# Attention feeding a mixture of experts on one core: batch loads over iterations, slot sums and lead products in another order, a separate home for late rows, two gathers sooner

## The chip, the core and the metric

The kernel runs on one core of a Trainium2 chip. The metric is the device time of one execution in microseconds. The engines named below are TensorE (PE; its weight loads are shown as PEld), VectorE (DVE), ScalarE (ACT), GpSimd (Pool) and SyncE (SP), which here only issues DMAs.

## What is computed

A chunked linear attention with decay, over 4 batches, 8 heads, 768 positions, whose output goes, row by row, to one of 8 experts. Cut to what matters:

```python
# attention, per batch and head, chunk by chunk
cum = cumsum(log(a))
y = (C @ B.T * exp(cum_i - cum_j) * causal) @ x + (C @ state) * exp(cum)
state = exp(sum(log a)) * state + sum_j(B_j x_j * exp(cum_last - cum_j))
# mixture of experts over the 3072 rows of 256 of y
logits = y @ w_gate                  # 256 x 8
e = argmax(logits); gate = softmax(logits)[e]
slot = rows so far that chose e      # kept if below the capacity of 768
out[row] = gate * (relu(y[row] @ w1[e]) @ w2[e])   # 256 -> 1024 -> 256
```

## The kernel before

The order of the instructions of every engine is written out by hand; engines wait for each other by semaphores that the framework sets from the tiles that they read and write. A tile pool gives a buffer again when its last readers are done, and memory of a pool that is closed goes to pools opened later, whose tiles then wait for the old ones' readers.

**Attention** (up to L874) works on 24 tiles of 128 positions, six per batch, in the loop over `k`. Iteration `k` makes the score products of tile `k` (`scores`, L441, from `b_n` and `cbd`, a block form of `c_n`) and masks them, turns the finished rows of tile `k - 2` (`rows_of`, `stage_c`: transposes L480, logits L484, copies to `rt` L498 and of the logits L485), multiplies tile `k - 1` (`intra` L462, `inter` L473) and carries the state (`carry` L401). The loads of batch `b + 1` are spread over the six iterations of batch `b` by `load_part(b + 1, t)` (L341), all on SP's queue: at `t = 0` `bt` and `cn`, at `t = 1` `bn` and the first part of `x`, at `t = 2` six loads of decay rows (L220) and four of blocks of `cn` into `cbd` (L353), at `t = 3` the second part of `x`. `paced` (L337) makes a load wait for the decay product of the next tile. `make_bp(k + 2)` reads `b_s`, `make_ct(k + 2)` reads `c_n`. From iteration 10 on SP also loads the raw weights of experts 0 and 1.

**Routing** is done for groups of tiles (4, 4, 4, 4, 4, 3, 1): `route_1` on DVE finds the best expert, `route_2` counts on TensorE, `route_3` makes slot numbers and one-hot matrices (`hot_a`, `hot_e`, `hot_b`), and `listed` or `list_` (L832) sums row numbers into the table of slots. `who` (L851) is the finished table. `rt` rows with the gate behind them go to DRAM, `rows_d` (L577).

**The lead** is a block of 128 rows of expert 0, known after the first 12 tiles and gathered during attention. At attention's end it is turned (`lead_turn`, L621: two transposes L156, each followed by a copy L625) and multiplied by expert 0's `w1` in four products of 8 matmuls (`lead_gemm`, L630, matmuls L636, Relu L637): one before the last groups' counts, one behind the first `list_`, two before the last `list_`. Its second product is L1100, and eight matmuls of no use (L1105) fill the time behind it.

**Experts** (`experts`, L883) run in eight units; unit 0 is the rest of expert 0 (296 rows), the others have 424. Rows are fetched by indirect DMAs on Pool in blocks of 128 (`gather`, L893, `fetch`, L169) into buffers `g`, three of them in the pool `gp`, which is opened when attention's pools are closed. Unit 0's three blocks are fetched at once; unit 1's four one by one, the block `f` after the matmuls of column block `f` of unit 0's first product (`gemm1`, L983, L990). Then `turned` transposes the rows of the next unit on TensorE (units 0 and 1) or on DVE (the others), between the two products of the unit before (`gemm2`, L1007). `hp` holds `hh` and `hl`, the two halves of the intermediate; `hl`'s buffer holds `x` of batches 0 and 2 during attention. The gate of a row is read in `put` (L1040) from column 256 of `g`. Weights of the expert after next are loaded behind matmuls of `gemm1`.

## Time and profile before

| what | us |
|---|---|
| median of 3 runs | 272.77 |
| lowest, highest | 272.13, 274.0 |
| the profiled execution | 274.5 |
| its span, first to last instruction | 272.6 |
| TensorE busy | 250.5 (92%) |
| DVE, Pool, ACT busy | 177.0, 130.4, 128.1 |

The profile is of one execution. Its rows name an engine, a line of the kernel and what an instruction writes and reads, as `ps<-xh,wh`. "Idle before" is time in which the engine did nothing ahead of an instruction, with what released it. "issue" marks time in which the engine waited for nothing that the profile shows. [...] Busy time of TensorE is modelled and holds pipelined matmuls.

### The profile page before, as it was taken

Reading aid. Unit: us, or ns where it says so; the run is one execution under the profiler, and the core shown is the slowest. Engines: PE = TensorE matmul, PEld = TensorE weight load, DVE = VectorE, ACT = ScalarE, POOL = GpSimd, SP = SyncE. Lnnn points to the kernel's source line nnn. Section 1 sums busy time; section 2 is a strip of 40 time slices with the busy share of each in tenths; the row PEclk is TensorE's granted clock in tenths of the full one; section 3 lists DMA queues with packets and bytes.
Section 4 is the critical chain, followed back from the end, with each engine's and each line's share of the span. In section 5 each row is a group of like instructions: output and inputs, shape, how many; then the busy total and the mean of one; then the engine's idle time right before and its main releaser. Section 6 shows DMA issues by size and latency. Waiting matters only on the chain.

```text
span 272.6 us, 7096 instructions
## 1 busy us (share of the span) xinstructions
PE 250.5 (92%) x2747; PEld 208.3 (76%) x2747; DVE 177.0 (65%) x437; ACT 128.1 (47%) x289; POOL 130.4 (48%) x165
## 2 busy tenths in 40 slices
PE   7799999969999996979999999999999999999960
PEld 3246556635557884979999999999999999999960
DVE  6699597846896852565686587478488676766210
ACT  2377457547755251455373373274284554643000
POOL 6975234324691232634466567467444475015230
PEclk9999999986999598999999999999999999999996
DMA  6583536935746401494762773773865815101010
GB/s 190 163 248 91 149 113 196 308 84 126 195 148 189 155 10 38 150 363 160 205 256 86 181 297 101 192 302 112 243 242 147 356 41 166 36 2 62 20 43 5
DMA packets 30101, 42.06 MB, mean 154 GB/s; under 512 B 16089, under 2 KB 22075, under 8 KB 28528
## 3 DMA queue, kind: packets, MB, share of 16 engines
q1 hardware_dynamic: 26656, 33.69, 39.5%
q0 software_dynamic: 3280, 7.86, 9.2%
q8 instruction: 23, 0.38, 0.6%
q14 instruction: 14, 0.11, 0.2%
q10 hardware_dynamic: 128, 0.01, 0.0%
HBM read 32.19 MB, written 9.39 MB: 153 GB/s over the span
## 4 chain that ended last, share of the span: by engine, by line
PE 80%; DMA 6%; DVE 5%; issue 3%; ACT 1%; POOL 1%; POOLq 0%; SPq 0%; DVEq 0%
PE ps L983 26%; PE ps L1007 20%; PE sp L441 5%; PE yp L462 4%; PE ps2f L1065 4%; PE yp L473 3%; PE pj L480 3%; DMA r<-w 3%; DMA g<-rows_d,who 3%; PE dsp L401 3%; PE lead_p L636 2%; PE psy L1053 2%; PE ldp L391 2%; PE yp L411 1%; PE warm L304 1%
## 5 line engine op out<-in xcount | busy, mean ns | idle before, releaser
L169 POOL DMA_INDIRECT g<-rows_d,who x31 | 49.9, 1610 | 44.4 <-PE ps L1007 31.7
L986 DVE SCALAR_TENSOR_TENSOR hl<-ps,hh 128x424 fp32r<-128x424 f32 (+1 forms) x64 | 37.1, 582 | 32.3 <-ACT hh L985 32.3
L985 ACT ACTIVATE hh<-ps 128x424 fp32r<-128x424 f32 (+1 forms) x64 | 32.7, 512 | 46.4 <-PE ps L983 46.4
L1041 POOL DMA_INDIRECT out<-yo,oi x31 | 30.6, 987 | 33.1 <-DVE yo L1040 33.1
L1007 PE MATMUL ps<-hh,wh 128*128 128x424 f32 (+1 forms) x112 | 39.0, 348 | 0.0
L1007 PE MATMUL ps<-hh,wl 128*128 128x424 f32 (+1 forms) x112 | 38.8, 347 | 0.0
L1007 PE MATMUL ps<-hl,wh 128*128 128x424 f32 (+1 forms) x112 | 38.8, 347 | 0.0
L983 PE MATMUL ps<-xh,wh 128*128 128x424 f32 (+1 forms) x128 | 37.6, 375 | 0.2 <-ACT xh L945 0.2
L128 DVE TENSOR_TENSOR wl<-r,wh 128x1024 fp32r<-128x1024 f32 (+1 forms) x32 | 34.9, 1146 | 0.8 <-ACT wh L127 0.8
L983 PE MATMUL ps<-xh,wl 128*128 128x424 f32 (+1 forms) x128 | 35.3, 355 | 0.1
L983 PE MATMUL ps<-xl,wh 128*128 128x424 f32 (+1 forms) x128 | 34.7, 352 | 0.0
L127 ACT ACTIVATE wh<-r 128x1024 fp32r<-128x1024 f32 (+2 forms) x48 | 34.2, 765 | 0.1
L983 PEld LDWEIGHTS ps<-xh,wl 128*128 128x128 f32 x128 | 24.3, 194 | 1.3 <-DVE wl L128 0.7
L983 PEld LDWEIGHTS ps<-xl,wh 128*128 128x128 f32 x128 | 24.2, 192 | 0.6
L983 PEld LDWEIGHTS ps<-xh,wh 128*128 128x128 f32 x128 | 22.2, 194 | 0.8 <-ACT xh L945 0.4
L1007 PEld LDWEIGHTS ps<-hl,wh 128*128 128x128 f32 x112 | 21.1, 188 | 0.6
L1007 PEld LDWEIGHTS ps<-hh,wh 128*128 128x128 f32 x112 | 21.1, 188 | 0.4
L1007 PEld LDWEIGHTS ps<-hh,wl 128*128 128x128 f32 x112 | 21.0, 188 | 0.4
L475 ACT ACTIVATE ys<-yp 128x128 f32<-128x128 f32 x48 | 10.7, 275 | 20.7 <-PE yp L473 20.7
L447 DVE TENSOR_TENSOR mz<-sp,lx 128x512 f32<-128x512 f32 x24 | 16.5, 687 | 4.5 <-PE sp L441 4.0
L366 POOL TENSOR_TENSOR bpt<-b_s,wt 128x128 f32<-128x128 f32 x22 | 10.0, 456 | 17.5 <-PE dsp L401 17.4
L462 PEld LDWEIGHTS yp<-mz,xz 128*32 128x32 f32 x768 | 12.6, 112 | 5.4 <-issue 2.9
(185 smaller groups left out, 438.0 us busy)
## 6 DMA issues: line engine op xcount, KB each, us to landing
r<-w SPq DMA_DIRECT2D x12, 1024.0 KB, 6.1
r<-w SPq DMA_DIRECT2D x16, 256.0 KB, 4.0
g<-xr_d SPq DMA_DIRECT2D x24, 112.0 KB
rows_d<-rt SPq DMA_DIRECT2D x5, 514.0 KB
xr_d<-g SPq DMA_DIRECT2D x6, 385.5 KB
xz<-x SPq DMA_DIRECT2D x6, 256.0 KB, 4.2
b_s<-bt SPq DMA_DIRECT2D x3, 384.0 KB, 3.1
c_n<-cn SPq DMA_DIRECT2D x3, 384.0 KB, 3.8
```

The source lines that it names most:

```text
L127: act.activation(hi[:, sl], r[:, sl], AF.Copy)
L128: engine.tensor_tensor(out=lo[:, sl], in0=r[:, sl], in1=hi[:, sl].bitcast(F32), op=ALU.subtract)
L169: got = pool.indirect_dma_start(out=g[0:r, s], out_offset=None, in_=rows_d[0:known, :], in_offset=bass.IndirectOffsetOnAxis(ap=index[0:r, ...
L441: pe.matmul(sp[64 * c:64 * c + 64, g, 0:4 * CH], nat(b, "bn", ts.start, ts.stop)[gp], cbd[b % 2][gp, :, ts], start=True, stop=True)
L447: dve.tensor_tensor(out=m.rearrange("p (g h) i -> p g h i", g=2), in0=sp[:, :, 0:4 * CH].rearrange("p g (h i) -> p g h i", h=4), in1=lx.re ...
L462: step[0] = pe.matmul(yps[g][32 * hh:32 * hh + 32, c * CH:(c + 1) * CH], x_z[:, c, h * D:(h + 1) * D], m[:, h], start=c == 0, stop=False, ...
L983: mm = pe.matmul(ps, wv[:, k, fs], xv[:, k], start=i == 0, stop=i == 5)
L985: act.activation(hh[:, f, 0:w], ps, AF.Relu)
L986: dve.scalar_tensor_tensor(out=hl[:, f, 0:w], in0=ps, scalar=0.0, in1=hh[:, f, 0:w].bitcast(F32), op0=ALU.max, op1=ALU.subtract)
L1007: mm = pe.matmul(ps, wv[:, f, ds], hv[:, f, 0:w], start=f == 0 and j == 0, stop=f == NF - 1 and j == 2)
L1041: sc = pool.indirect_dma_start(out=out, out_offset=bass.IndirectOffsetOnAxis(ap=oi[0:r, s:s + 1], axis=0), in_=yo[0:r], in_offset=None, bo ...
L1065: pe.matmul(ps, hv[:, f, sl], wv[:, f, :], start=f == 0 and j == 0, stop=f == NF - 1 and j == 2)
```

## The change

In `load_part`, `cn` stays at `t = 0`, `bt` goes to `t = 1` and `bn` to the end of `t = 2`. In `stage_c`, for the tiles of the last two groups, the copies of the logits go ahead of the copy of the rows. `lead_turn` is called before the rows of tile 21 are turned, and its two copies are run after tile 23's `inter`; of the four lead products one stands ahead of the rows of tile 22, one ahead of the turn of the last tile, one where it stood behind the first `list_`, and one behind the counts (`cnt`). Unit 0's gathered rows get a tile in `hp` with the tag `hl`. The gate is copied to a small tile of its own in `turned`. Two of unit 1's four gathers are issued behind unit 0's, the other two behind column blocks 0 and 1.

```diff
--- before.py
+++ after.py
@@ -339,7 +339,7 @@
             follow(dma.ins, beat[0], "not all loads at once")
 
         def load_part(b, t):
-            for nm in ((("bt", "cn"), ("bn",)) + ((),) * 4)[t]:
+            for nm in ((("cn",), ("bt",)) + ((),) * 4)[t]:
                 paced(out=loads[b][nm], in_=src_of[nm][:, b])
             if t in (1, 3):
                 load_xz(b, t // 2, pace=True)
@@ -351,6 +351,7 @@
                     for g in range(2):
                         r = slice(64 * g + N * i, 64 * g + N * (i + 1))
                         sp_.dma_start(out=cbd[b % 2][r, i], in_=cn[r, b])
+                paced(out=loads[b]["bn"], in_=bn[:, b])
             if t in (3, 4):
                 expand(b, t - 3, 0, S, act)
 
@@ -495,8 +496,8 @@
                 r = lgs.shape[0]
                 pe.transpose(out=pj[:, 384:384 + r], in_=lgs, identity=ident[0:r, 0:r])
                 after.append(lambda: act.activation(Ls, pj[:, 384:384 + r].rearrange("p (j e) -> p j e", e=32)[:, :, 0:E], AF.Copy))
-            act.activation(rt[:, i, 0:DM], pj[:, 0:DM], AF.Copy)
-            for f in after:
+            late = [lambda: act.activation(rt[:, i, 0:DM], pj[:, 0:DM], AF.Copy)]
+            for f in after + late if direct else late + after:
                 f()
 
         def stage_c_last(ys, rt):
@@ -618,11 +619,11 @@
             numbers(lead_t["slot"], slice(0, 1))
             fetch(lead_t["g"], lead_t["slot"], lead, LEAD * P)
 
-        def lead_turn():
+        def lead_turn(stored):
             both = p1.tile([P, 2, 512], F32, name="lead_ps", tag="sp", bufs=2)
             banks = [both[:, k] for k in range(2)]
             turn(lead_t["g"], lead, lambda w: banks.pop(0)[:, 0:w],
-                 lambda k, ps: act.activation(lead_t["x"][:, k], ps, AF.Copy))
+                 lambda k, ps: stored.append(lambda: act.activation(lead_t["x"][:, k], ps, AF.Copy)))
             pool.tensor_copy(lead_t["gate"], lead_t["g"][:, 0, GATE:GATE + 1])
 
         lead_f = list(range(0, NF if lead else 0, 2))
@@ -788,19 +789,22 @@
         sb[k - 1] = inter(yps, cts.pop(k - 1), sa.pop(k - 1))
         for f in lots:
             f()
-        early = take()
+        early, stored = take(), []
+        if lead:
+            lead_turn(stored)
         rows_of(k - 2, k)
         early += take()
         yps, lots = intra(x_of(k), ms.pop(k), sa[k], None, hots)
         sb[k] = inter(yps, cts.pop(k), sa.pop(k))
         for f in lots:
             f()
+        for f in stored:
+            f()
         side.extend(early)
         settle_due(k + 1)
         early = take()
         assert not due and not hots
-        if lead:
-            lead_turn()
+        lead_gemm()
         rows_of(k - 1, k)
         mid = take()
         rt = sm.tile([P, 1, ROW], F32, name="rt_last", bufs=1)
@@ -809,6 +813,7 @@
             pe.matmul(lg, sb[k][:, g], wg[:, g, 0:E], start=g == 0, stop=g == 1, skip_group_check=True)
         last = route_last(k, rt, lg)
         late = take()
+        lead_gemm()
         pj = p1.tile([P, 512], F32, name="pj_last", tag="y")
         turn_rows(pj, sb.pop(k))
         act.activation(rt[:, 0, 0:DM], pj[:, 0:DM], AF.Copy)
@@ -819,7 +824,6 @@
         settled = sm.tile([P, E * ks], F32, name="settled")
         numbers(settled, slice(0, E * ks))
         weave(mid, [lambda: None, lambda: None] + late)
-        lead_gemm()
         mid = route_2(*due.pop()[1], at_of(1, 4 * E)[:, 0:3 * E].rearrange("p (t e) -> p t e", e=E))
         route_3(*mid)
         mid = take()
@@ -844,8 +848,6 @@
         hots.append(hot(*known[0], pool))
         hots.append(hot(*known[1], dve))
         known.clear()
-        while lead_f:
-            lead_gemm()
         while hots:
             list_(*hots.pop(0))
         dve.tensor_tensor(out=who, in0=settled, in1=spots, op=ALU.add)
@@ -853,6 +855,8 @@
         got = sm.tile([P, 2 * E], F32, name="got")
         for i, r in enumerate((runs[0], lead_run)):
             pe.matmul(cnt[:, i * E:(i + 1) * E], ones, r, start=True, stop=True)
+        while lead_f:
+            lead_gemm()
         act.activation(got, cnt, AF.Copy)
         most = sm.tile([P, 1], F32, name="most")
         late = sm.tile([P, 1], F32, name="late")
@@ -890,9 +894,9 @@
             ph = mt.enter_context(tc.tile_pool(name="ph", bufs=3, space=PSUM))
             py = mt.enter_context(tc.tile_pool(name="py", bufs=2, space=PSUM))
 
-            def gather(e, w0, w, most):
+            def gather(e, w0, w, most, home=None):
                 blocks = -(-w // P)
-                g = gp.tile([P, blocks, ROW], F32, name="g", bufs=3)
+                g = home.tile([P, blocks, ROW], F32, name="g_first", tag="hl") if home else gp.tile([P, blocks, ROW], F32, name="g", bufs=3)
 
                 def block(s, *pace):
                     fetch(g, who[:, e * ks + w0 // P:(e + 1) * ks], most, only=(s,), pace=pace)
@@ -958,7 +962,11 @@
                     act.activation(xh, xt[:, :, 0:w], AF.Copy)
                     dve.tensor_tensor(out=xl, in0=xt[:, :, 0:w], in1=xh.bitcast(F32), op=ALU.subtract)
                 if not rare:
-                    gate = g[:, :, GATE]
+                    gate = gp.tile([P, -(-w // P)], F32, name="gate")
+                    full = w // P
+                    for s0, n, r in ((0, full, P), (full, 1, w % P)):
+                        if n and r:
+                            dve.tensor_copy(gate[0:r, s0:s0 + n], g[0:r, s0:s0 + n, GATE])
                 gone = dead[:, e]
                 if rare:
                     gone = gp.tile([P, -(-w // P)], I32, name="gone")
@@ -1084,13 +1092,16 @@
             size = lambda u: units[u][2] if u < 2 else -(-units[u][2] // Q) * Q
             g, g_n, now = None, None, []
             if not rare:
-                g, now = gather(*first, size(0))
+                g, now = gather(*first, size(0), hp)
             for job in now:
                 job()
             ahead_g, four = {}, {}
             if len(units) > 1:
                 ahead_g[1], more = gather(*units[1], size(1))
                 rows_.extend(more)
+            if not rare:
+                for _ in range(2):
+                    rows_.pop(0)()
             after = []
             if ahead:
                 yt = gp.tile([P, 2, lead], F32, name="yt", bufs=1)
```

## Rows read from the trace of the kernel before

**Rows 1.** The page, part 4: the chain that ended last, by engine.

```profile
PE 80%; DMA 6%; DVE 5%; issue 3%; ACT 1%; POOL 1%; POOLq 0%; SPq 0%; DVEq 0%
```

**Rows 2.** The chain in order of time, attention; columns: start us, us, what.

```profile
34.80 0.59 PE sp L441 x8
...
54.64 0.59 PE sp L441 x8
...
56.66 2.52 issue
...
68.48 0.59 PE sp L441 x8
```

**Rows 3.** Stretches: length; busy PE, PEld, DVE, ACT, POOL; clock; DMA share, GB/s.

```profile
47.00:56.00 9.00, 9.00 (x224) 5.44 (x226) 7.32 (x25) 5.36 (x19) 3.16 (x8) 1.00 0.94 282
...
57.00:58.00 1.00, 0.00 (x0) 0.00 (x0) 0.21 (x2) 0.00 (x0) 0.16 (x1) 1.00 0.05 7
58.00:59.00 1.00, 0.00 (x0) 0.00 (x0) 0.00 (x0) 0.00 (x0) 0.00 (x0) 1.00 0.08 12
...
59.20:66.00 6.80, 6.80 (x104) 3.63 (x104) 3.06 (x12) 3.98 (x13) 1.67 (x4) 0.50 0.53 133
...
90.00:96.70 6.70, 6.24 (x40) 5.85 (x40) 4.59 (x32) 1.36 (x5) 1.03 (x3) 0.50 0.29 98
103.00:106.30 3.30, 1.38 (x6) 0.75 (x6) 0.00 (x0) 0.42 (x1) 0.94 (x1) 1.00 0.18 52
107.00:110.00 3.00, 3.00 (x13) 3.00 (x14) 1.27 (x6) 0.46 (x2) 1.03 (x1) 0.50 0.01 3
...
117.00:118.00 1.00, 0.48 (x4) 0.44 (x4) 0.00 (x0) 0.20 (x1) 0.00 (x0) 1.00 1.21 361
```

**Rows 4.** The page, part 3: the queue that brings instructions.

```profile
q8 instruction: 23, 0.38, 0.6%
```

**Rows 5.** Timeline of DVE: start us, us, line, op; what ended its idle time.

```profile
94.55 0.33 DVE L596 TENSOR_TENSOR hot_b<-hot_e,cb_s 128x48 bf16<-128x48 bf16 x2
97.37 0.20 DVE L851 TENSOR_TENSOR who<-settled,spots 128x48 int32<-128x48 f32 x1 [2.50 <-PE cnt L855]
...
98.73 0.15 DVE L869 TENSOR_TENSOR load<-late,most 128x1 int32<-128x1 f32 x1
```

**Rows 6.** Timeline of TensorE, attention's end and expert 0.

```profile
46.26 0.74 PE L441 MATMUL sp<-cbd,b_n 64*64 64x256 f32 x8
...
91.94 5.17 PE L636 MATMUL lead_p<-lead_h,r 128*128 128x128 f32 x24
...
97.68 3.83 PE L1100 MATMUL ps<-lead_h,r 128*128 128x128 f32 x32 [0.33 <-ACT got L856]
101.34 1.62 PE L1105 MATMUL warm<-cb_s 128*128 128x432 bf16 x8
...
106.86 0.60 PE L983 MATMUL ps<-xh,wh 128*128 128x296 f32 x1 [0.15 <-ACT xh L945]
...
115.16 0.81 PE L156 MATMUL ps<-hd_s,g 128*128 128x128 f32 x3
117.52 0.92 PE L156 MATMUL ps<-hd_s,g 40*128 40x40 f32 x5 [1.55 <-DMA g<-rows_d,who]
```

**Rows 7.** Timeline of Pool: first gather of expert 0, last of expert 1.

```profile
99.74 1.60 POOL L169 DMA_INDIRECT g<-rows_d,who  x1 [5.29 <-ACT wh L127]
...
112.80 0.99 POOL L169 DMA_INDIRECT g<-rows_d,who  x1 [0.30 <-PE ps L983]
```

**Rows 8.** Timeline of SP's DMA queue in attention.

```profile
40.03 2.01 SPq L353 DMA_DIRECT2D cbd<-cn  x4
...
50.84 0.46 SPq L338 DMA_DIRECT2D b_n<-bn  x1
```

**Rows 9.** The DMA issues by line: count, KB each, median us to landing.

```profile
c_n<-cn SPq DMA_DIRECT2D x3, 384.0 KB, 3.8
...
xz<-x SPq DMA_DIRECT2D x6, 128.0 KB, 6.8
```

## The prediction

> **What bounds the kernel now.** I read the page first: the chain of work that ended last is TensorE for 80% of the span [rows 1], so a change pays only where TensorE stands still or runs at the lower of its two clock levels. Then I looked for such places, in the chain in order of time, in the table of stretches, and in the timelines of the engines around each. There are three.
>
> The first is in attention. Score products start on average every 2.83 us: from 34.80 to 54.64, seven iterations, 19.84 us. The next three take from 54.64 to 68.48, 13.84 us, where 3 x 2.83 = 8.49 were due: 5.35 us are lost [rows 2]. Of these, 2.52 us are a standstill marked "issue", in which TensorE waits for no semaphore. In the nine microseconds before it the DMA engines are 94% busy; in it they do almost nothing (7 and 12 GB/s) [rows 3]. 7 plus 12 KB is about one packet of the "instruction" queue: 0.38 MB in 23 packets is 16.5 KB each [rows 4]. I read this as code that TensorE is short of, whose transfer had stood behind the data until they were through. After it the clock is 0.50 (1.2 GHz) from 59.2 to 66 us [rows 3]; the other 5.35 - 2.52 = 2.83 us (by chance the same figure) are put down to that.
>
> The second place is the end of attention. DVE has the last one-hot product ready at 94.88 (94.55 + 0.33), but `who`, the table of which row sits in which expert's slot, is added only at 97.37 [rows 5], because 24 matmuls of the lead block stand before the last slot sums in TensorE's order, from 91.94 [rows 6]. The gather of expert 0's rows begins later still, at 99.74 [rows 7]. Its target lies in memory that attention's pools have to give back, and the last instruction that reads one of those small tiles is `load<-late,most`, which ends at 98.88 [rows 5], 0.86 us before. TensorE runs out of work, is busy for 1.38 of 3.30 us, and falls to 0.50 for the first matmuls of expert 0 [rows 3].
>
> The third is between the two products of expert 0: the turn of expert 1's rows starts at 115.16, and its last block, whose gather began at 112.80, is there at 117.52, after 1.55 us of waiting [rows 6, 7]. From 118.4 on TensorE is full, one expert after the other; what is won before stays won unless weights or rows are late.
>
> **The change, part by part.** The profiled execution took 274.5 us (span 272.6); the median of the runs is 272.77, 1.7 less. The terms are differences, taken from the profiled execution and subtracted from the median.
>
> *Loads spread.* At the batch's first iteration `cn` is loaded alone, `bt` moves to the second, where `bn` was, and `bn` to the third, behind six row loads and four block loads on SP. Nothing is added or removed: three loads of 384 KB per batch. What changes is the heap that the code packet stands behind. Before, `bt` and `cn` were issued together and `bn` behind them at 50.84 [rows 8]; afterwards `bt` goes there, and one load of 384 KB fewer is ahead. At the 282 GB/s of that stretch [rows 3] this is 1.36 us; I take 1.2, since part of the time was less than full. The standstill falls from 2.52 to about 1.3 us. An idle of 1.55 us before 117.52 left the clock at 1.00 [rows 3, 6], so at 1.3 us I take it as kept, and the 2.83 us come back too: 4.0 us. The ends are 0 (the heap does not matter) and 5.35 (no standstill).
>
> [...] The row says that the packet came only when the data were through [rows 3]. [...]
>
> What this costs: `bn` is late by design. In batch 1 the block loads end at 42.04 [rows 8]; `bn` goes next, and the like-sized `cn` lands 3.8 us after issue [rows 9], thus at 45.9; the first product that reads it starts at 46.26 [rows 6]. That is no slack to speak of. By the 6.8 us of the slowest kind of load [rows 9] it would be at 48.9 and TensorE would stand 2.6 us. I take the near row and charge 0.3 us for all three batches (ends 0 and 2.6 for each of two). Stores of rows, `x` and weights queued behind it on SP start 0.4 us later and have more slack than that.
>
> *Slot sums ahead of lead products.* The four lead products (8 matmuls each) are spread: one before the rows of tile 22 are turned, one before the last tile's, one where it was, one after the counts. At the higher clock 32 such matmuls take 3.83 us [rows 6], so a product is 0.96; at the lower, 24 in 5.17, so 1.72. The routing chain on DVE has one product ahead of it that was not there, and two small copies on ACT; the copy of the logits now goes ahead of the copy of the rows, which gives a part back. I charge the chain 1.0 us (ends 0 and 1.9): the last one-hot at 95.9 instead of 94.88, `who` complete at 96.45 instead of 97.57. The slot sums no longer queue.
>
> *A home of their own.* Expert 0's gathers go into the `hl` buffer, free since batch 2's `x` was used, and so wait for `who` and the stored rows only. With Pool's 0.86 us from release to start, the first begins at 97.3 instead of 99.74: 2.4 us earlier, and the last block is there at 105.55 - 2.4 = 103.1. TensorE's own work: counts at 96.2, a lead product 0.96, 0.33 of waiting for ACT, then 3.83 and the filler 1.62 [rows 6], thus 102.9. Both sides meet, so I take 2.4 (ends: 0 with TensorE late, 3.0).
>
> With no gap there is no fall of the clock. From 106.86 to 115.16 stand 48 matmuls and two small ones, 8.30 us [rows 6]; of this 3.0 us at least run at 0.50 [rows 3]. Work at half the clock takes twice its time, so half of the 3.0 would come back, 1.5; I take 1.3, as a short gap may be left (ends 0 and 1.7).
>
> *Expert 1's gathers forward.* Two of four follow expert 0's three directly, the others after the first and second column block of its first product instead of the third and fourth. Pool does the same gathers in the same order. The last leaves some 2.5 us earlier in relation to the product, before expert 1's weights are asked for. The 1.55 us of waiting go; it can't give more (lower end 0). The later blocks then queue behind nothing on Pool.
>
> *Gate copies.* Two small DVE copies per unit, some 0.15 us each like those of [rows 5], lie beside matmuls; DVE is busy for 177.0 of 272.6 us: 0. Without that cover they would cost 8 x 0.3 = 2.4 us. They set the gathered rows free one unit earlier.
>
> Sum: -4.0 + 0.3 - 2.4 - 1.3 - 1.55 = -8.95 us; 272.8 - 8.95 = 263.8 us.
>
> **The rivals.**
>
> *The heap does not matter.* The code packet is late for another reason, or is served in turn with the data and simply asked for late, and the 5.35 us stay. For it: a standstill named "issue" has no releaser in the profile. Against: it lies right behind the fullest nine microseconds of attention [rows 3]. The time is 263.8 + 4.0 = 267.8. [...]
>
> *Lead products run at the lower clock.* Before, the clock was 0.50 from 90 to 96.7 us [rows 3]. If it falls likewise, one product costs the chain 0.76 us more, the one after the counts 0.76 more, and the 32 matmuls up to 3.1 more: TensorE is ready at 107.5 instead of 102.9, 2.0 us behind where the last rows came before. Then 2.4 are not won but 2.0 lost: 268.2. Against it: two of the four now stand before 90 us, where it fell, and make TensorE's work there denser.
>
> *`bn` late* (the other side). If its transfer lands after 6.8 us instead of 3.8, batches 1 and 2 both begin with about 2.6 us of standstill, and each pulls the clock down as at 59 us, another 2.83: 2 x 5.4 = 10.9 us against 9.25 won, thus 272.8 - 9.25 + 10.9 = 274.4. It turns the sign from a landing of 6.0 us on; from 7.4 us on, 0.6 more in each of the two batches, the time is over 275.5. For it: its place on SP; against it: `cn` of the same size lands in 3.8 us [rows 9].
>
> *Given back.* Experts 2 to 7 have to wait for weights by what was won: 272.8. Against it: those loads are issued after matmuls, and so move with them.
>
> **How the numbers follow.** Forecast 0.52; heap 0.20 (the cause is read from two rows, not from a releaser); lower clock 0.12; given back 0.07; `bn` late 0.09, two thirds of it with the longer landing, as standstills add up. The number is that of the forecast. Its own range is 261.5 to 266: the low end is no standstill at all (1.35 more) and 3.0 for the home (0.6 more), 261.9 and a little; the high end is half of one of the large terms gone. The first two rivals, at 267.8 and 268.2, are taken in, with one microsecond on top: 261.5 to 269.5 leaves the last two out, and some of the others' tails. About 1% is what a measurement can tell from no change: faster than 270.0 are the first three, 0.84; within 1% "given back" and a third of `bn` late, 0.10; slower the rest of that, 0.06.
>
> **What would show it.** Right: a chain with no or a shorter "issue" piece near 56 us and a clock of 1.00 there; `bn` loads landed before scores of tiles 6, 12 and 18; `who` near 96.5 and the first gather within 1 us of it, both moved by what attention gains; no lower clock in expert 0's first product; no wait for DMA at expert 1's turn. Wrong: a standstill as long as before; a gather that still starts behind `load<-late,most`; lead products at 1.7 us each; a new wait for `b_n`; a wait for weights behind expert 1.

## The result: 1.1% faster, a third of what was forecast

The changed kernel takes 269.52 us (median of 20 runs, 268.27 to 274.97), the kernel before in the same runs 273.07. The ratio of the times is 0.9887, 95% interval 0.9855 to 0.9919, so 3.1 us where 8.95 were forecast; 269.52 lies just above the range. In two later jobs the ratio was 0.9878 and 0.989. All ratios are to the kernel before in the same job. (Of most kernels here some executions show a lower mean clock and are longer, of the changed one four of 20 with 0.947 to 0.959 and 273.33 to 274.97 us; ratios, and averages over "undisturbed" profiles, leave them out, medians do not.)

The profiled execution took 269.67 us, span 267.9. Its chain by engine, to be held against [rows 1]:

```profile
PE 80%; DVE 7%; DMA 3%; issue 3%; ACT 2%; POOL 1%; SPq 0%; POOLq 0%; ACTq 0%; DVEq 0%
```

The chain in order of time, attention (start us, us, what), against [rows 2]:

```profile
24.55 4.12 DMA b_n<-bn
28.80 0.78 PE sp L442 x8
...
46.30 1.15 issue
...
52.76 1.36 issue
...
69.93 0.45 issue
...
85.75 0.48 issue
```

The standstill at 56.66 is gone, but four shorter ones stand elsewhere, and `bn` is on the chain, which it was not. They add up to 3.4 us against 2.52 before (a piece of 0.75 to 0.87 near 75, which both have, left out).

The one at 46.30 ends with the first score product of tile 12, which reads the `bn` loaded for its batch:

```profile
42.53 1.04 SPq L338 DMA_DIRECT2D b_n<-bn  x1
...
47.42 0.36 PEld L442 LDWEIGHTS sp<-cbd,b_n 64*64 64x64 f32 x8 [1.21 <-issue]
```

No view names its releaser, but the trace's semaphore records do: the semaphore of this load makes its last step at 47.36, 0.06 us before the weight load. So 1.15 of the 3.4 us are a wait for `bn`, and the other three pieces, 2.3 us, stand against the 2.52 of before.

TensorE at the end of attention and in expert 0, against [rows 6]:

```profile
95.52 2.05 PE L637 MATMUL lead_p<-lead_h,r 128*128 128x128 f32 x8
98.12 5.23 PE L1111 MATMUL ps<-lead_h,r 128*128 128x128 f32 x32 [0.55 <-ACT got L860]
103.19 1.62 PE L1116 MATMUL warm<-cb_s 128*128 128x432 bf16 x8
104.65 1.12 PE L156 MATMUL ps<-hd_s,g_first 128*128 128x128 f32 x6
105.72 0.95 PE L991 MATMUL ps<-xh,wh 128*128 128x296 f32 x2
...
113.04 1.33 PE L156 MATMUL ps<-hd_s,g 128*128 128x128 f32 x8
114.30 0.41 PE L1015 MATMUL ps<-hh,wh 128*128 128x296 f32 x1
```

DVE, against [rows 5]:

```profile
95.05 0.33 DVE L597 TENSOR_TENSOR hot_b<-hot_e,cb_s 128x48 bf16<-128x48 bf16 x2
95.67 0.20 DVE L853 TENSOR_TENSOR who<-settled,spots 128x48 int32<-128x48 f32 x1 [0.29 <-PE cnt L857]
99.19 0.15 DVE L873 TENSOR_TENSOR load<-late,most 128x1 int32<-128x1 f32 x1
```

Pool's gathers, against [rows 7]:

```profile
97.27 1.07 POOL L169 DMA_INDIRECT g_first<-rows_d,who  x1 [2.32 <-issue]
...
99.95 1.15 POOL L169 DMA_INDIRECT g_first<-rows_d,who  x1 [0.30 <-DVE lead_oi L876]
...
108.80 0.99 POOL L169 DMA_INDIRECT g<-rows_d,who  x1 [0.30 <-issue]
```

Stretches (length; busy PE, PEld, DVE, ACT, POOL; clock; DMA share, GB/s), against [rows 3]:

```profile
88.00:94.20 6.20, 4.79 (x50) 4.38 (x49) 5.91 (x42) 2.08 (x8) 1.07 (x3) 1.00 0.35 117
94.20:101.10 6.90, 5.74 (x32) 5.29 (x32) 4.17 (x19) 2.53 (x6) 3.97 (x5) 0.51 0.28 88
...
105.00:113.00 8.00, 7.85 (x55) 7.35 (x55) 4.90 (x16) 3.75 (x9) 2.85 (x3) 1.00 0.36 103
```

The gathers begin at the time that was forecast (97.3), no longer behind `load<-late,most`, and neither expert's turn waits for a row. That it is just this time is luck: it was to move with attention, which gained 0.65 us, and from the end of `who` (95.87) to the first gather it is 1.40 us where 0.86 were taken. And TensorE is late: the clock is 0.50 from 94.2 to 101.1 (a share of the full clock; no trace here shows it in GHz), two lead products pay for it, and expert 0's rows are turned only at 104.65.

Cut at four points, the two profiled executions differ as follows; the rows below the first are distances between neighbouring points. The last tile's score product and expert 0's first product, before:

```profile
82.98 0.66 PE L441 MATMUL sp<-cbd,b_n 64*64 64x256 f32 x8
...
106.31 0.40 PE L983 MATMUL ps<-xh,wh 128*128 128x296 f32 x1
```

and the last tile's score product after:

```profile
82.33 0.66 PE L442 MATMUL sp<-cbd,b_n 64*64 64x256 f32 x8
```

```
stretch                                          before   after   differs  forecast
start to the last tile's score product            82.98   82.33    -0.65     -3.7
  to expert 0's first product                     23.33   23.39    +0.06     -2.4
  to the turn of expert 1's rows                   8.85    7.32    -1.53     -1.3
  to expert 0's second product                     3.20    1.26    -1.94     -1.55
  to the end of the time                         156.14  155.37    -0.77      0
```

Nearly all that is missing in these two executions lies in the first two lines, 3.05 and 2.46 us. The experiments ask why.

### The profile page after: what moved, and what is told of

Its sections match the earlier page's. It is cut to its first block, busy times and chain, and to the rows that moved or that the text cites. A ratio compares the mean times of both kernels' runs of the same rounds, so it can differ in the third digit from the quotient of the medians.

```text
span 267.9 us, 7098 instructions
## 1 busy us (share of the span) xinstructions
PE 246.7 (92%) x2746; PEld 206.3 (77%) x2747; DVE 178.6 (67%) x453; ACT 127.6 (48%) x289; POOL 126.5 (47%) x165
## 4 chain that ended last, share of the span: by engine, by line
PE 80%; DVE 7%; DMA 3%; issue 3%; ACT 2%; POOL 1%; SPq 0%; POOLq 0%; ACTq 0%; DVEq 0%
PE ps L991 27%; PE ps L1015 23%; PE sp L442 4%; PE ps2f L1073 4%; PE yp L463 4%; PE yp L474 3%; PE pj L481 2%; PE psy L1061 2%; PE dsp L402 2%; PE ps L1111 2%; DMA b_n<-bn 2%; PE ldp L392 1%; DMA c_n<-cn 1%; DVE mz L448 1%; PE yp L412 1%
## 5 line engine op out<-in xcount | busy, mean ns | idle before, releaser
L169 POOL DMA_INDIRECT g<-rows_d,who x28 | 42.7, 1527 | 37.3 <-PE ps L1015 32.6
L991 PE MATMUL ps<-xh,wh 128*128 128x424 f32 (+1 forms) x128 | 36.9, 368 | 0.1
L991 PE MATMUL ps<-xh,wl 128*128 128x424 f32 (+1 forms) x128 | 34.2, 348 | 0.0
L991 PE MATMUL ps<-xl,wh 128*128 128x424 f32 (+1 forms) x128 | 34.1, 348 | 0.0
L991 PEld LDWEIGHTS ps<-xl,wh 128*128 128x128 f32 x128 | 23.6, 188 | 0.7
L991 PEld LDWEIGHTS ps<-xh,wl 128*128 128x128 f32 x128 | 23.6, 188 | 0.6
L991 PEld LDWEIGHTS ps<-xh,wh 128*128 128x128 f32 x128 | 21.6, 189 | 0.8 <-ACT xh L949 0.4
L448 DVE TENSOR_TENSOR mz<-sp,lx 128x512 f32<-128x512 f32 x24 | 16.5, 686 | 5.3 <-PE sp L442 3.7
L442 PE MATMUL sp<-cbd,b_n 64*64 64x256 f32 x176 | 15.5, 401 | 2.0 <-issue 1.6
```

The source lines that it names most:

```text
L169: got = pool.indirect_dma_start(out=g[0:r, s], out_offset=None, in_=rows_d[0:known, :], in_offset=bass.IndirectOffsetOnAxis(ap=index[0:r, ...
L442: pe.matmul(sp[64 * c:64 * c + 64, g, 0:4 * CH], nat(b, "bn", ts.start, ts.stop)[gp], cbd[b % 2][gp, :, ts], start=True, stop=True)
L448: dve.tensor_tensor(out=m.rearrange("p (g h) i -> p g h i", g=2), in0=sp[:, :, 0:4 * CH].rearrange("p g (h i) -> p g h i", h=4), in1=lx.re ...
L991: mm = pe.matmul(ps, wv[:, k, fs], xv[:, k], start=i == 0, stop=i == 5)
```

## Experiments on the loads

**The kernel before once more, and each half alone.** No edit in the first. In the second, the kernel before with only the loads spread:

```diff
-            for nm in ((("bt", "cn"), ("bn",)) + ((),) * 4)[t]:
+            for nm in ((("cn",), ("bt",)) + ((),) * 4)[t]:
...
                         sp_.dma_start(out=cbd[b % 2][r, i], in_=cn[r, b])
+                paced(out=loads[b]["bn"], in_=bn[:, b])
```

In the third, the changed kernel with the reverse edit.

> The kernel before, unchanged, for a second profiled execution. Theory: the 2.52 us standstill at 56.66 and the lower clock behind it were one draw of when a packet of TensorE's code got through the full DMA queue, not a fixed cost of the bunched loads. Then this execution shows a standstill of another size or at another place, and the score product of the last tile (82.98 in the first profile) starts 1 to 3 us away from that. Rival (the bunched loads cost this each time): again a standstill of over 2 us between 54 and 59, TensorE at the lower clock behind it, the last tile's score product within 0.7 us of 82.98. Either way expert 0's second product starts 35 to 39 us behind that score product, and the total is 271 to 277 us.

> The kernel before with only the loads spread (cn, then bt, then bn behind the ten row and block loads). Theory: the spread trades one wait for others; the late bn holds the first score product of tile 12 for about 1.2 us and that of tile 6 for 0.5, and what stands behind it on SP makes a later code packet late; score products of the last tile start within 1 us of the 82.98 us of before, total 0 to 1.5 us less than before. Rival (the prediction's own term): the standstill and the lower clock go and bn costs 0.3: total 3.7 us less.

> The changed kernel with the loads in the order of before. Theory: attention as before, with its one standstill near 56 us and the lower clock behind it; the end of attention and expert 0 keep their gain of about 3.5 us, so 0 to 1 us slower than the changed kernel. Rival: the loads are worth 3.7 us, so 3 to 4 us slower than the changed kernel, no faster than before by more than 1 us.

Measured: the second execution of the kernel before took 275.15 us, and its chain shows

```profile
67.69 1.27 issue
...
84.10 1.50 issue
```

and no piece over 0.5 us near 56. Its last score product starts at 80.89, 2.1 us sooner, and yet it takes as long: expert 0's first product follows 25.13 us behind, against 23.33. Held against this execution the first two lines of the table would be +1.44 and -1.74 us; how the loss divides between them is a draw too, and what both comparisons share is their small sum, -0.3 and -0.6 us. So the 2.52 us of [rows 2] were one draw, as the theory said. Loads alone: 275.48 us against 272.38 for the kernel before, ratio 1.015 [0.981, 1.050], too wide to tell a gain from a loss. The changed kernel with the old loads: 270.20, ratio 0.9895 [0.981, 0.998], as much as with the new ones in their job.

Why does the standstill wander? I paired the transfers of the "instruction" queue with TensorE's instructions: packet k is asked for at instruction 249k and needed at 249(k+1), all of TensorE's records counted, nearly all of them weight loads and matmuls. This pairing is my estimate from the records, not a row of the profile. For the 249: in the first profiles of both kernels 250 records on average lie between the starts of two packets, from the first packet to the 22nd. For "needed": the standstill of 2.52 us in the kernel before ends at record 2241, 9.0 times 249, those of 1.36, 0.45 and 0.48 us in the changed kernel at 1984, 2752 and 3520, 7.97, 11.05 and 14.14 times. For "asked": in these two profiles every packet but the last starts between 1 record ahead of 249k and 249 behind it, from 99 us on 9 to 61 behind; what asks for a packet no record shows. The pairing fits in that the standstills marked "issue" of over 0.4 us between 26 and 92 us end 1.2 to 1.8 us behind the end of such a packet, in all profiles. The exceptions are waits ahead of tile 12, like the one at 46.30: in the five profiles that have one, all with spread loads, it ends 0.1 us behind the landing of `bn`. Times in us; "spread" says how the loads are ordered, "weights" whether expert 1's first weight loads are issued in tile 22; "standstill" is the longest distance at the second place between the starts of two neighbouring matmuls (some 0.2 us more than the idle time of a row).

```
                              near 52 to 57           near 78 to 84
kernel         spread weights asked  starts  later    asked  starts  later  standstill
before         no     yes     51.5   56.7    5.2      81.8   82.8    1.0    0.67
before again   no     yes     51.9   54.9    3.0      79.7   83.3    3.6    1.71
old loads      no     yes     51.7   55.0    3.3      78.4   82.0    3.6    1.59
loads only     yes    yes     53.2   56.1    2.9      79.7   83.5    3.8    1.99
after          yes    yes     54.4   57.2    2.8      81.1   83.7    2.6    0.70
late weights   yes    no      54.7   56.7    2.0      80.8   82.6    1.8    0.61
weights later  no     no      52.6   55.7    3.1      79.6   81.0    1.4    0.61
```

The first draw of the kernel before had the longest wait, 5.2 us, near 56; none of the others here has over 3.3, and no further profile over 3.8. At the other place, where the weights are in, the packet starts between 82.0 and 83.7 in these five whether it was asked for at 78.4 or at 81.8. A kernel that comes there sooner waits longer: what attention has won is given back. (0.61 to 0.67 is a wait for ACT that every execution has there.) A packet has 16,384 bytes in the trace, in line with the 16.5 KB worked out from [rows 4]; by the pairing TensorE stood for one by up to 2.5 us at a time (2.52 in the first profile of the kernel before).

**`bn` at the head of its iteration**, ahead of the row and block loads.

```diff
             if t == 2:
+                paced(out=loads[b]["bn"], in_=bn[:, b])
                 for q in range(3):
...
-                paced(out=loads[b]["bn"], in_=bn[:, b])
```

> The changed kernel with bn at the head of its iteration, ahead of the six row loads and four block loads instead of behind them. Theory: bn is there long before tiles 6 and 12, the waits of 0.5 and 1.2 us go, and rows, x and weights leave SP as before: 1 to 2.5 us faster than the changed kernel. Rival: the wait at tile 12 is not for bn but for code, and stays: within 0.5 us of the changed kernel.

Measured: 267.58 us, ratio 0.9917 [0.987, 0.997]. In its trace tile 12 waits for nothing, as the theory of a wait for `bn` said and the rival (code) did not, but tile 6 waits 1.88 us for the block loads, and the last score product starts at 81.05. One load was traded for another; whether it gains time was not settled.

**Weights behind the last rows' stores.**

```diff
             if k == TILES - 2:
-                raw_home(1)
-                for i in range(4):
-                    load_weights(1, i, 4, paced)
...
         hots.append(hot(*known[1], dve))
+        raw_home(1)
+        for i in range(4):
+            load_weights(1, i, 4, sp_.dma_start)
```

> The changed kernel with expert 1's first four weight loads (256 KB each) issued behind the last rows' stores instead of in tile 22. Theory (what attention wins earlier is given back at the code packet that TensorE needs near 82 us, which stands behind row stores and these weights): that packet comes in time, no standstill of over 0.5 us between 81 and 86, no lower clock until the idle stretch at 94, so expert 0's second product starts 1 to 2 us sooner than otherwise at the same start of the last score product (32.0 us behind it in the changed kernel, 36 with the lower clock), and the median is 265.5 to 268 us against 269.5 of the changed kernel. Rival 1 (the weights do not hold the packet; row stores and tile 23's own loads do): the standstill of 1.2 to 2 us stays, and the time is within 1 us of the changed kernel's. Rival 2 (the weights are missed later): expert 1's first product waits for them near 120 us, 1 to 3 us slower than the changed kernel.

Measured: no standstill over 0.61 us in that place, and the lower clock comes only at 94.1, as the theory said; but the median is 269.19 us, ratio 0.9926 [0.987, 0.998], no better than the changed kernel's 269.52 and 0.9887 of another job; the profiled execution of that had one of the short standstills (0.70) anyway. In six profiles with late weights, those further below among them, this place shows 0.61 to 0.64; in the fourteen with the weights in tile 22, 0.64 to 2.53. In the eight of these with 1.59 or more the clock fell between 85.7 and 90.8; with late weights it fell behind this place at 91.1 at the earliest. A long standstill is not the only way to an early fall: in the first profile of the kernel before (0.67) it fell at 89.8.

## Experiments on the end of attention

**Without the useless products** (eight matmuls into `warm`, ahead of expert 0's rows; the output does not depend on them).

```diff
-                warm = py.tile([P, CBW], F32, name="warm", tag="ps2")
-                for _ in range(8):
-                    pe.matmul(warm, ones, cb_s[:, 0:CBW], start=True, stop=True)
```

> The changed kernel without the eight matmuls of no use behind the lead's second product. Theory: in the changed kernel the rows of expert 0 are there before TensorE is (it is held up by the lead products at the lower clock), so the turn starts at about 103.3 instead of 104.65 us: 1.3 us faster. Rival: the rows are not there, or the clock falls in expert 0's first product without the filler: same or up to 1.5 us slower.

Measured: 267.67 us, ratio 0.9905 [0.984, 0.997]. The rows of expert 0 are there without a wait at 22.16 us behind the last score product, against 22.33 with the products: the lower clock came earlier, at 90.7, and took their 1.6 us.

**More useless products, to hold the clock** (`fill(n, ...)` issues n matmuls of 256 columns).

```diff
+        fill(5, "yp1")
         for op in early:
             op()
...
         lead_gemm()
+        fill(14, "yp1")
         weave(mid[3:], late)
```

> The changed kernel with 19 more useless products of 256 columns (5 ahead of the last selections, 14 behind the first list) in the place where TensorE otherwise has nothing between 88 and 95 us. Theory (the clock fell to 0.50 from 94.2 to 101.1 because TensorE had nearly nothing to do there, and the second lead product pays for it): the granted clock stays at 1.00 to 101, lead product 4 takes 0.96 us instead of 2.05, the second lead product of 32 takes 3.83 us instead of 5.23, expert 0's rows are turned round 2 us sooner, at 102.4 to 102.9 instead of 104.65 for the same start of the last score product, and the median is 1.5 to 2.5 us under the changed kernel's 269.5. Rival (the clock falls from what went before, not from the want of work): it falls all the same, the added products take 0.21 us each at half speed, 3 to 4 us together, and the time is 0 to 2 us over the changed kernel's.

TensorE in its trace:

```profile
95.52 1.14 PE L637 MATMUL lead_p<-lead_h,r 128*128 128x128 f32 x8
97.21 3.84 PE L1118 MATMUL ps<-lead_h,r 128*128 128x128 f32 x32 [0.55 <-ACT got L867]
...
102.34 0.38 PE L156 MATMUL ps<-hd_s,g_first 128*128 128x128 f32 x2
103.68 0.81 PE L156 MATMUL ps<-hd_s,g_first 40*128 40x40 f32 x4 [0.96 <-DMA g_first<-rows_d,who]
```

and its stretches:

```profile
88.00:94.20 6.20, 6.00 (x63) 5.56 (x62) 5.91 (x42) 2.10 (x8) 1.06 (x3) 1.00 0.34 117
94.20:101.00 6.80, 6.23 (x59) 5.76 (x57) 5.00 (x20) 2.81 (x7) 3.74 (x5) 1.00 0.25 75
...
106.20:109.60 3.40, 3.40 (x16) 3.40 (x15) 1.40 (x3) 1.03 (x3) 1.98 (x2) 0.50 0.20 46
```

Busy for 6.00 instead of 4.79 of the 6.20 us before 94.2, TensorE keeps the full clock, both lead products have their full speed, and the turn comes 1.9 us sooner behind the last score product. So the cause of the slow lead products, the lower clock behind that stretch, is shown. Yet expert 0's second product starts 32.59 us behind that score product, against 31.98: now the rows are late, by 0.96 us, and the clock falls behind that wait. The profiled time was 269.9; three further executions took 274.6 to 277.0, of which no trace exists. The ratio on record, 1.0215 [1.009, 1.034], rests on those, so the times decide nothing. By the trace the theory's mechanism stands, and its 2 us do not come.

**The order of before for slot sums and lead products.** `lead_turn` stands behind the last selections again, two products together behind the lists' start, the copy of the rows ahead of that of the logits; of its edits:

```diff
-            for f in after + late if direct else late + after:
...
-        lead_gemm()
+        if lead:
+            lead_turn()
...
         hots.append(hot(*known[1], dve))
         known.clear()
+        while lead_f:
+            lead_gemm()
         while hots:
             list_(*hots.pop(0))
```

> The changed kernel with the order of before for the slot sums and the lead pairs: lead_turn behind the last selections, both lead products together behind the lists, and the row copy ahead of the logits' copy. Theory (the slot sums' list, last hot_b to the first gather, wins 1.5 to 2 us by that order, and it is seen only where TensorE is not the later one): the instruction `who` starts 1.5 to 2 us later relative to the last score product (13.3 us behind it in the changed kernel, 14.4 in before), and the second lead product runs at full clock (3.8 us); expert 0's rows are turned round within 0.5 us of where they are in the changed kernel, and the median is within 1 us of it. Rival (the spread order is worth its 2 us to the end): 1.5 to 3 us slower than the changed kernel.

Measured: 273.31 us, ratio 1.0146 [1.009, 1.020]; in the same job the kernel with late weights took 269.19 and the kernel before, by its median, 273.57. DVE:

```profile
97.71 0.33 DVE L597 TENSOR_TENSOR hot_b<-hot_e,cb_s 128x48 bf16<-128x48 bf16 x2
100.79 0.20 DVE L852 TENSOR_TENSOR who<-settled,spots 128x48 int32<-128x48 f32 x1 [2.75 <-PE cnt L856]
```

The wait of 2.75 us for the queue of lead products is back, so the spread order is worth its place. What it is worth in time is not clean: this execution had 2.53 us of standstill near 84 and a clock of 0.50 from 86.7 to 100.4.

**Expert 1's gathers paced as before, and expert 0's gathers in the old buffers.**

```diff
-            if not rare:
-                for _ in range(2):
-                    rows_.pop(0)()
...
-                g, now = gather(*first, size(0), hp)
+                g, now = gather(*first, size(0))
```

The first hunk is the one kernel, the second the other; beside them ran the changed kernel again.

> The changed kernel with expert 1's four gathers paced by expert 0's column blocks as before. Theory (the gathers forward are worth their 1.55 us): expert 1's last block is there 1.3 to 2 us after TensorE wants it, the wait for a DMA of g stands again in the turn of expert 1's rows, expert 0's second product starts 33.3 to 34 us behind the last score product instead of 32.0, and the median is 1 to 2 us over the changed kernel's. Rival (with expert 0 started earlier Pool has the time anyway): no wait over 0.4 us at that turn, and within 0.7 us of the changed kernel.

> The changed kernel with expert 0's gathers in the same buffers as those of the other experts, as before. Theory (the target's memory held the first gather back): the first gather starts behind the instruction that writes load from late and most, 2.4 us behind `who` instead of 1.6, and the second one 1.9 us behind the first instead of 1.4; expert 0's rows are there 1.2 to 1.8 us later, TensorE, which is ready 9.0 us behind `who`, waits 0 to 1 us for them, and the median is 0 to 1 us over the changed kernel's. Rival (the home is worth 2.4 us by itself): 2 to 3 us over the changed kernel's, with a standstill and a lower clock in expert 0's first product.

> The changed kernel, unchanged, for a second profile and as the measure for the others. Theory (attention loses about the same in standstills whatever the order of the loads, at places that differ from one execution to the next): the standstills over 0.8 us before the last score product and the three microseconds behind it add up to 3 to 5 us again, but not at the places of the first profile (46.14, 52.48, 69.56); expert 0's second product starts 32 us behind the last score product where no standstill over 1.5 us lies at 83 to 85, and 35 to 36 us where one does. Rival (the late `bn` and the code packets have fixed costs): the same places, each within 0.3 us. Median 268.5 to 271.

Measured: the changed kernel 271.65 us, ratio 0.9878 [0.983, 0.992]; late gathers 281.70; old home 274.33, ratio 1.0017 [0.994, 1.010]. TensorE with late gathers:

```profile
121.78 0.58 PE L156 MATMUL ps<-hd_s,g 128*128 128x128 f32 x2
124.73 0.33 PE L156 MATMUL ps<-hd_s,g 128*128 128x128 f32 x1 [2.37 <-DMA g<-rows_d,who]
```

From the turn to the second product it takes 5.03 us instead of 1.26, and behind the standstill the clock falls from 125.0 to 131.8: the rest of the time is 157.74 instead of 155.4. Together 6 us, more than either theory had; in the kernel before, with the same pacing, the stretch was 3.20 us. Its four executions took 276.46 to 284.55 us, too few and too far apart for a ratio, so the size is rough; the wait is a row. Pool with the old home:

```profile
100.24 1.52 POOL L169 DMA_INDIRECT g<-rows_d,who  x1 [5.33 <-DVE wl L128]
```

This is 0.94 us behind the end of `load<-late,most` (99.15 + 0.15) and 4.6 us behind `who`, against 1.6 in the changed kernel, but TensorE, at the lower clock, waits only 0.46 us for the rows. In the traces the home is worth 0.7 us to expert 0's second product (32.69 against 31.98), by the ratios 1.4% or 3.8 us: between the two theories, and not settled. In the second trace of the changed kernel, an execution of 275.06 us, the standstills were indeed elsewhere (28.29, 56.03, 62.66), but `bn` held tile 6 again, for 3.12 us, and tile 12 for 0.55: the same two tiles, other amounts.

## The edits together, and the loads once more

The first kernel has late weights and no useless products; the next four ran together on one chip: this one and the changed kernel, each with spread loads and with the loads of before.

> The changed kernel without the 8 useless products ahead of expert 0's rows and with expert 1's first weight loads behind the last rows' stores. Theory (each took one loss away: 1.6 us of useless products in TensorE's order, and the code packet near 82 us that stood behind weights): both add up, expert 0's second product 31.5 to 32 us behind the last score product with no lower clock before 90, and a median of 266 to 267.5 us, under both kernels. Rival (what one saves the other gives back, as the rows of expert 0 are the later side then): expert 0's rows are waited for by 0.5 to 1.5 us at their turn, and the median is that of the changed kernel within 1 us.

> The changed kernel with the loads of before, without the 8 useless products, and with expert 1's first weight loads behind the last rows' stores. Theory (the spread loads cost 0.4 to 3.4 us at tile 6 and save nothing): tile 6's score product waits for no load, the last score product starts 79 to 81 us, expert 0's second product 31.5 to 32.5 behind it, and the median is 265.5 to 267.5 us, 1 to 2 under the same kernel with spread loads. Rival (the spread loads are worth up to 4 us): the median is 2 to 4 us over the same kernel with spread loads, with a standstill of over 2 us near 56.

> The same kernel with the loads spread as in the change (run once before, 268.57 with four runs). Theory: a wait of 0.4 to 3.4 us at tile 6 again, median 267 to 269, 1 to 2 us over the kernel with the loads of before. Rival: median 2 to 4 us under it.

> The changed kernel with the loads of before (270.20 in another job). Theory: no wait at tile 6, the last score product at 79 to 83 us, median 268 to 270, 0.5 to 2 us under the changed kernel in this job. Rival (the spread loads bring up to 4 us): 2 to 4 us over the changed kernel.

> The changed kernel beside the other three. Theory: a wait of 0.4 to 3.4 us for bn at tile 6 in its profile, median 269.5 to 271.5. Rival: no such wait, and the lowest median of the two without the other edits.

Measured: the first kernel 268.57 us, ratio 0.9837 [0.979, 0.989], by the ratios 1.1 us under the changed kernel of the same job (0.9878), with overlapping intervals; by the medians 3 us. It has a second product 30.03 us behind the last score product, though expert 0's rows are now waited for by 0.7 us: both theories in part. Then, with the kernel before at 273.18:

```
                               loads spread               loads of before
changed kernel                 272.94  0.989 [.982,.997]  269.86  0.986 [.980,.992]
late weights, no filler        267.29  0.978 [.973,.984]  266.50  0.977 [.971,.982]
```

The old loads are not the worse ones in either line, but the intervals overlap: the spread loads bring nothing that can be seen, against 4.0 forecast (1.5%, which both lines shut out); whether they cost something the times leave open. The traces say where they may. With them, tile 6 waits for a load in eleven of twelve executions, as in the first kernel:

```profile
29.88 0.78 PE L442 MATMUL sp<-cbd,b_n 64*64 64x256 f32 x8 [1.37 <-DMA b_n<-bn]
```

With the old loads it waits in none of seven. Over the nine undisturbed profiles with spread loads this wait is 0.70 us on average (0 to 1.37). Little of it is lost: tile 7's score product starts at 31.89 on average, against 31.73 in the five with the old loads, which stand near 31 instead (the kernel before for 0.35 us at 30.85). The wait at tile 12, in three of the nine (1.15, 0.87 and 0.33 us), stays: tile 13 starts at 49.30 against 48.86. The last score product starts at 81.72 on average against 80.57, but with ranges that overlap (80.21 to 82.70, 79.13 to 82.98) and other edits are mixed in.

**Weights later still.** Without useless products and with the old loads, the weights issued only behind the first sum of the second lead product; beside it, the same kernel with the weights behind the row stores.

```diff
-        raw_home(1)
-        for i in range(4):
-            load_weights(1, i, 4, sp_.dma_start)
...
+                    if d == 0:
+                        raw_home(1)
+                        for i in range(4):
+                            dma = load_weights(1, i, 4, sp_.dma_start)
+                            follow(dma.ins, mark.ins.name, "rows first")
```

> The changed kernel with the loads of before, without the 8 useless products, and with expert 1's first weight loads issued on SP only behind the first of the two sums of the second lead product. Theory (the weights behind the row stores hold the first gather up): it starts 1.0 to 1.7 us behind `who`, expert 0's turn waits for no row, expert 0's second product starts 30.0 to 31.0 us behind the last score product (31.5 where the weights follow the row stores), and the median is 0.7 to 1.5 us under that of the kernel beside it. Rival (the gather is held by something else): it starts 2.7 to 3.1 us behind `who` as before, and the medians agree within 0.5 us.

> The same kernel with the weights right behind the row stores (266.50 in another job). Both theories: the first gather 2.7 to 3.1 us behind `who`, no standstill over 0.7 us at 80 to 86, no wait at tile 6, median 266 to 267.5 us.

Measured: 266.12 us, ratio 0.981 [0.974, 0.988], against 265.41, ratio 0.984 [0.978, 0.989]. Pool's first gather, weights later still:

```profile
95.01 1.08 POOL L169 DMA_INDIRECT g_first<-rows_d,who  x1 [2.37 <-DMA rows_d<-rt_last]
```

and with the weights right behind the stores:

```profile
94.66 1.07 POOL L169 DMA_INDIRECT g_first<-rows_d,who  x1 [3.67 <-DVE dead L862]
```

The first starts 1.67 us behind `who` (93.34), the second 2.96 behind it (91.70): the weights did hold up the gather, which waits for the last rows' store. No row is waited for any more, but the second product starts only 0.45 us sooner behind the last score product (30.37 against 30.82), and the times agree. Here too TensorE, with its lead products at 0.50 from 93.5 to 100.3, is the later side.

## Why the forecast was wrong

*Loads spread (-4.0 forecast, none found).* This step failed, mechanism and size. It took one execution's standstill for a cost of the bunched loads. The second execution had none there, and others of 1.27 and 1.50 us later. So the sign named for being right, no long "issue" piece near 56 and a clock of 1.00 there, came by luck: the second execution of the kernel before shows it too. The 5.35 us themselves were too large: in the last kernel above with the old loads (265.41 us), which has no standstill over 0.4 us there, the three iterations priced at 8.49 take 9.58. Code packets wait with either order of the loads (1.7 to 3.8 us near 55, beside the one of 5.2), and a kernel that is early at one of them can be late by more at the next. The first rival had the right amount, 0, for this term. Whether its mechanism is right stays open: in what order the DMA engines served the code packet and the data was not shown. For the weights the heap does matter: with 1 MB of them in, the packet of the table's second place waits 1.0 to 4.2 us over all profiles, without them 1.4 to 2.0, and only with them does TensorE stand there for it (0.64 to 2.53 us, against 0.61 to 0.64 with the wait for ACT alone). Which packets it stood behind no record shows.

*`bn` late (+0.3).* The right mechanism, too small. The load was taken to land 3.8 us after its issue, like `cn`; by the semaphore records of the changed kernel's trace the three take 4.12, 4.83 and 3.85 us. Tile 12, whose load is the one that the working followed from 42.04, stood for 1.15 us. Tile 6 stood for 0.39; for it the same row-by-row sum would have been: block loads end at 24.6, 3.8 us to land, 28.4, against 28.31, where this product starts before; no slack at all. Together that is 1.54 us where 0.3 was charged, though the 0.39 is made up by tile 7 (31.57, before 31.59). The new wait for `b_n` was a sign named for being wrong. The rival of that name, 2.6 us in two batches with a fall of the clock, had the two batches right and not the sizes; no fall followed.

*Slot sums ahead of lead products (right).* `who` starts 13.34 us behind the last score product instead of 14.39, 1.05 sooner where 1.12 was forecast (15.91 in the second execution of the kernel before).

*A home of their own (-2.4 forecast, +0.06 measured).* This step failed too: right for Pool, wrong for TensorE. The last gather of expert 0 starts 17.63 us behind the last score product (at 99.95) instead of 19.96, 2.33 sooner; before:

```profile
102.94 0.99 POOL L169 DMA_INDIRECT g<-rows_d,who  x1 [0.30 <-issue]
```

But the step let "both sides meet" with lead products at full speed. The two behind the counts took 2.05 and 5.23 us instead of 0.96 and 3.83, 2.5 us together, and that is what is missing in this pair of executions. This is the second rival, "lead products run at the lower clock", with its 2.0 us. Its counter-argument, that two products stand earlier and make the work denser, was not enough: TensorE was busy for 4.79 of the 6.20 us before the clock fell.

*Clock kept in expert 0's first product (-1.3 forecast, -1.53 measured)* and *expert 1's gathers forward (-1.55 forecast, -1.94 measured)*: right. For the first the forecast reckoned twice the time at half the clock; the matmuls of the lead products start 213 ns apart at 0.50 and 112 at 1.00 in the kernel before, 1.9 times as far. Undone alone, the gathers cost more than that in the one trace, probably since the pacing ties them to a product that now starts without a gap.

*Given back by the later experts:* no; they won another 0.77 us, which was not forecast and was not traced further.

## What to carry to other kernels

A standstill with no releaser should be seen in a second execution before it is priced: its place here moved by tens of microseconds between executions of one kernel. Nor is every "issue" the same: of the four in the changed kernel's chain three follow a code packet and one a load, told apart by what lands just before they end. What an earlier stage wins is not won until the next fixed arrival is passed; here that was, by the pairing, a code packet with 1 MB of weights in the queue, and asking for the weights later took the standstill away (0.61 to 0.64 us in that place instead of up to 2.53). Where two engines meet at one point, cost both sides at the clock that the stretch before leaves them, not at the best one.

The best of these kernels had the loads of before, no useless products and expert 1's first weights behind the row stores: 266.50 us (ratio 0.977) and 265.41 (0.984) in two jobs, against 0.989 for the change as it was made.

## What the runs showed that was not expected

Packets of TensorE's code, 16,384 bytes each, started in attention up to 5.2 us after the instruction that I take to ask for them, and TensorE stood for up to 2.5 us. Useless products that kept the clock at 1.00 through one gap moved the fall to the next one, 106.2 to 109.6, with no time won.
